# A third tile of an expert with at most 64 rows, run as 64 rows with both parts in one stationary block

## The chip, the core and the metric

The kernel runs on one core of one Trainium2 chip. The metric is the device time in microseconds (us) of one execution, as the median of several runs. The engines are called PE (TensorE: matmuls, with PEld its weight loads), ACT (ScalarE), DVE (VectorE), POOL (GpSimd) and SP (SyncE, which here issues DMAs). Each has a queue of its own and takes its instructions in order; they wait for each other through semaphores. A matmul multiplies a stationary block (up to 128 x 128) with a moving block of up to 512 columns and adds the result up in PSUM.

## What is computed

A clustered attention (8 heads, 2 batches, 768 tokens, 64 values per head: each query sees only the keys of its own cluster), and on its 1536 result rows of 512 values a mixture of 8 experts with a hidden layer of 1024. Each row goes to the expert of its largest logit; an expert takes at most 384 rows (capacity). Cut to the second half:

```python
logits = x @ w_gate                       # x: 1536 x 512, w_gate: 512 x 8
expert_idx = np.argmax(logits, axis=1)
# row i is put at the next free place of its expert's queue, if there is one
h = np.maximum(np.einsum('ecd,edf->ecf', disp, w1), 0.0)     # 512 -> 1024
y = np.einsum('ecf,efd->ecd', h, w2)                         # 1024 -> 512
out[i] = gate_w[i] * y[expert_idx[i], pos[i]]
```

How many rows an expert gets depends on the data. In the input that is timed, the eight counts are 198, 119, 169, 188, 162, 192, 206 and 302.

## The kernel before

Products are made to near float32 precision by splitting each operand into two 12-bit parts, high and low, and adding three products: high x high, high x low and low x high. So each block of an expert's product is three matmuls.

An expert's rows lie in up to three tiles of 128 rows (`ST` = 3). Two of them (`MT` = 2) are always computed, together: `gemm1` makes the hidden layer in 8 groups (one for each `f`, 12 matmuls of 256 columns each, weights stationary, lines 733 to 748), `gemm2` makes the result of one tile of 128 rows (24 matmuls of 512 columns, the hidden layer stationary, line 674). The third tile is wanted only by an expert with more than 256 rows; it stands behind a branch on the count (line 831) and is computed by `single`: 4 transposes of the rows (`turn`, line 644, with ACT at line 646 writing the high part and DVE at line 647 the low one), 24 matmuls of 512 columns for the hidden layer (line 702, with the rows as the stationary block), two turns of the hidden layer (4 transposes each), 24 matmuls for the result (line 674), and `finish`: DVE scales the rows with the gate's weight (line 667), and POOL scatters them to the output (line 527). Expert 0 is special: its first tile is closed early and computed before the routing is done, so it has a fourth tile, and two branches. In the timed input only expert 7 has a third tile, with 302 - 256 = 46 rows; all other branches are passed over.

The counts are fetched into registers of all engines by `values_load` (line 813), one load per expert and engine. The weights come in chunks of 0.5 MB by DMA and are split by ACT (line 126) and DVE (line 132); `w_next` does so between the groups of matmuls.

The order of the work in the experts' part is that of a scheduler, within the stretches between barriers. It also places the branches: that of an expert stands, in PE's queue, between the expert's `gemm1` and its `gemm2`. The seven loads of the counts of experts 1 to 7 follow behind the two branches of expert 0 and 24 more matmuls.

Of the kernel before, what the change touches and what calls it, by code (L numbers as in the profile page):

```python
# [7 lines left out]
F32 = mybir.dt.float32  # L8
R32 = mybir.dt.float32r
BF16 = mybir.dt.bfloat16  # L10
I32 = mybir.dt.int32
AF = mybir.ActivationFunctionType
ALU = mybir.AluOpType
# [3 lines left out]
P = 128  # L17
BIG = float(2 ** 60)
# [5 lines left out]
def kernel(  # L24
# [13 lines left out]
    nc = tc.nc  # L38
    B, NP, _, S = qT.shape
# [65 lines left out]

    # ---- expert weights: 0.5 MB chunks, each split into two 12-bit parts
    slots = [wra.tile([P, 2, 1024], R32, name=f"ws{c}") for c in range(NA)]
# [25 lines left out]

    # Scores are two products, K = 112 and 97: W x Y1 and Qs x Y0.
    #   main rows:  q_hi x k_hi              | q_hi x k_lo
    #   piece rows: q_lo x k_hi, d 0-31      | q_lo x k_hi, d 32-63
    #   last rows:  query x key cluster mask | -(row maximum) x 1
    # for heads of parity 0; mirrored for parity 1, whose rows 16-31 and 1-31 are zero
    MAIN = (slice(0, 64), slice(64, 128))
# [32 lines left out]

    # ---- cluster assignment of the two heads of a pair -> 0/1 rows for W, 0/-BIG rows for Y1
    cl = {}
# [15 lines left out]
    def cl_scores0(nm, t0=0, t1=NT):  # L190
        # first pair: centroids as they came, all heads' at once; each product leaves its own 32 columns
        # and the next one writes over the rest
        if t0 == 0:
            cl[0, nm] = psS.tile([P, 512], F32, tag="s", name="ctp")
        for t in range(t0, t1):
            nc.tensor.matmul(
                out=cl[0, nm][:, t * 32:(t + NP) * 32],
                lhsT=pair[0][nm][:, t * P:(t + 1) * P],
                rhs=cbr,
                start=True,  # L200
                stop=True,
            )

    def cl_assign(pi, mul=nc.gpsimd, norm=None, nm="qk"):
        # token x (tile, q/k, head) groups; pair 0: one call each for q and k
        G = NT * 2 * len(nm)
        tv = (cl.pop(pi) if norm is None else cl.pop((pi, nm)))[:, 0:G * 16]
        if norm is not None:
            sn = work.tile([P, NT * 4, 16], F32, tag="csn", name="csn", bufs=2)[:, 0:G]
            nc.vector.tensor_tensor(  # L210
                out=sn.rearrange("p (t g) c -> p t (g c)", g=2),
                in0=tv.rearrange("p (t c) -> p t c", c=32),
                in1=norm.to_broadcast([P, NT, 32]),
                op=ALU.mult,
            )
            tv = sn
        else:
            tv = tv.rearrange("p (g c) -> p g c", c=16)
        mx = work.tile([P, NT * 4, 1], F32, tag="cmx", name="cmx")[:, 0:G]
        nc.vector.tensor_reduce(out=mx, in_=tv, axis=AX.X, op=ALU.max)  # L220
        yield
        eq = work.tile([P, NT * 4, 16], BF16, tag="ceq", name="ceq", bufs=2)[:, 0:G]
        nc.vector.tensor_tensor(out=eq, in0=tv, in1=mx.to_broadcast([P, G, 16]), op=ALU.is_equal)
        c16 = c16b.rearrange("p (o c) -> p o c", o=1)
        mul.tensor_tensor(out=eq, in0=eq, in1=c16.to_broadcast([P, G, 16]), op=ALU.mult)
        yield
        m2 = work.tile([P, NT * 4, 1], BF16, tag="cm2", name="cm2")[:, 0:G]
        nc.vector.tensor_reduce(out=m2, in_=eq, axis=AX.X, op=ALU.max)
        yield
        # the groups of 16 (q even, q odd, k even, k odd head) go to columns 0, 32, 64, 96  # L230
        g0, ng = 2 * "qk".index(nm[0]), 2 * len(nm)
        ov = ohb.rearrange("p t (g c) -> p t g c", c=32)[:, :, g0:g0 + ng, 0:16]
        nc.vector.tensor_tensor(
            out=ov,
            in0=eq.rearrange("p (t g) c -> p t g c", g=ng),
            in1=m2.rearrange("p (t g) o -> p t g o", g=ng).to_broadcast([P, NT, ng, 16]),
            op=ALU.is_equal,
        )
# [28 lines left out]

    # ---- exact split of q and k into two 12-bit parts
    ql = {}
# [25 lines left out]

    # ---- row maxima of the masked scores, per query
    mxt = {}
# [24 lines left out]
    def max_part(h, j, pool=psO, tag="o"):  # L322
        # maxima of half the queries, transposed one tile at a time
        mx = work.tile([P, TH], F32, tag="mxp", name="mxp")
        ts = slice(j * TH, (j + 1) * TH)
        nc.vector.tensor_tensor(out=mx, in0=mxt[h][:, 0, ts], in1=mxt[h][:, 1, ts], op=ALU.max)
        br = MROW[h % 2]
        tp = pool.tile([P, 512], F32, tag=tag, name="mtd")
        if j == 0 and h == 0:
            keep_warm(WARM2, tp)  # L330
        for t in range(TH):
            nc.tensor.transpose(tp[0:1, t * P:(t + 1) * P], mx[:, t:t + 1], ident)
        nc.scalar.activation(
            out=pick(Qs_t, h)[br:br + 1, j * HALF:(j + 1) * HALF], in_=tp[0:1, 0:HALF], func=AF.Copy, scale=-1.0
        )
        if j == 1:
            mxt.pop(h)
# [10 lines left out]

    # ---- attention proper
    pt = {}  # L350
# [78 lines left out]

    # ---- routing: expert, gate weight, position in the expert's queue; rows go to their slots  # L430
    run = []

    def gate(b, t0=0, t1=NT):
# [18 lines left out]
        yield  # L452
        # positions in the queues, and positions + first rows of the experts' slots
        ps = psT.tile([P, 512], F32, tag="t", name="gps")
# [4 lines left out]

        # earlier rows of the same tile, earlier tiles, earlier calls  # L460
        o2 = oh.rearrange("p (o t) e -> p o (t e)", o=1).to_broadcast([P, 2, n * E])
# [6 lines left out]
        nc.tensor.matmul(out=pv, lhsT=oneb, rhs=spread(run[-1], n), start=False, stop=True)  # L468
        # gate weight of the largest logit: 1 / (sum exp(l - max) + 1e-9)
        ex = tl("gex")  # L470
        nc.vector.tensor_tensor(out=ex, in0=lg, in1=mx.to_broadcast(sh), op=ALU.subtract)
        nc.scalar.activation(out=ex, in_=ex, func=AF.Exp)
        # slot out of range when the expert is full
        v, w = tl("gv"), tl("gw")
# [11 lines left out]
        for t in range(n):  # L486
            scatter("xd", xd, si[:, t], xt[b][:, t0 + t, :], (E * ST + 1) * P - 1)
        # tokens of each expert so far, per row
        cnew = tl("gcu", E, F32, 1)[:, 0]
# [8 lines left out]
    def first_rows():  # L498
        # expert 0's first tile takes no rows after this: later ones start at its second
        ebr, dlr = (const.tile([P, E], BF16, name=n) for n in ("ebr", "dlr"))  # L500
        nc.vector.memset(ebr, 0.0)
        nc.vector.memset(dlr, 0.0)
        nc.vector.tensor_copy(ebr[0:1], cs[0:1, C_EB:C_EB + E])
        first.append(ebr)
        run0 = const.tile([P, E], BF16, name="run0")
        nc.vector.memset(run0, 0.0)
        run.append(run0)
        first.append(dlr)
# [16 lines left out]
    def scatter(key, dst, idx, src, bound):  # L525
        # rows of one call never meet those of another: no order among the calls
        i = nc.gpsimd.indirect_dma_start(  # L527
# [26 lines left out]
    def hooks(i, g):  # L554
# [13 lines left out]
        if i == 0:  # L568
# [4 lines left out]
            if g in (2, 3, 4, 5):  # L573
                split(2, g - 2)
        # work for other heads between the groups of head i
        n = i + 1
# [39 lines left out]

    # ---- experts
    def moe(tail):
# [20 lines left out]
        def turn(src, hi, lo, pool, tag):  # L639
            # [rows, n * 128] -> n blocks of [128, rows], in two 12-bit parts  # L640
            tp = pool.tile([P, 512], F32, tag=tag, name="rtp")
# [39 lines left out]

        # one tile of 128 rows: both products with the rows stationary, the hidden layer turned between them
        def single(e, t, sfx, pools):
# [28 lines left out]
            for f in range(KF):  # L712
# [4 lines left out]
                gemm2_step(ps, e, f, h[0], h[1], slice(0, P))  # L717
            finish(e, t, ps, sfx)

        hf0 = []  # L720
# [50 lines left out]
        for e in range(E):  # L771
# [58 lines left out]
            for t in range(2 if e == 0 else MT, T0 if e == 0 else ST):  # L830
                with tc.If(n_e[e] > t * P):  # L831
                    for _ in single(e, t, "c", one):
                        pass

    def keep_warm(n, d):
        # the tensor engine's clock rises only while it is busy; nothing reads these products
        for _ in range(n):
            nc.tensor.matmul(out=d[:, 0:P], lhsT=onef, rhs=onef, start=True, stop=True)

    def centroid_scale():  # L840
        # 1 / (|c| + 1e-6) on every partition; the root is refined by one Newton step
        nc_ = NP * 32
# [144 lines left out]
def _prepare(inputs):  # L987
# [12 lines left out]
    t["v1"] = vv  # L1000
    # centroids, block-diagonal for the two heads of a pair
    cp = c.reshape(H // 2, 2, 16, D)
# [46 lines left out]
```

## Time and profile before

| | us |
|---|---|
| median of 3 runs | 513.41 |
| lowest and highest run | 513.39, 515.55 |
| profiled execution: span from first to last instruction | 508.1 |
| PE busy in it | 478.8 |
| DVE busy in it | 376.2 |
| ACT busy in it | 318.2 |
| POOL busy in it | 149.5 |

The span is that of one profiled execution; the device time has 5.3 us more, which lie outside of it. The experts' part is the last 200 us or so of the span. A row of a time line gives the start and the duration of an instruction, its engine and its line; several alike in a row are one row with a count (x2), and the duration is then that of all. Matmuls overlap: one of 512 columns is shown with 0.39 us, and the next starts 0.23 us behind it. In square brackets stands the idle time of the engine ahead of it, and what ended it. `PEq` is PE's sequencer, which also does loads of registers and branches.

### The profile page before, as it was taken

The page shows a single profiled execution, that of the slowest core. Times are in us where ns is not written, and L with a number is a line of the kernel's source. Part 1 is how long each engine was busy: PE and PEld are TensorE (multiplying, and loading weights), DVE is VectorE, ACT ScalarE, POOL GpSimd, SP SyncE. Part 2 cuts the span into 40 slices and gives each one's busy share as a digit, 9 for nine tenths or more (in the row PEclk, how much of TensorE's full clock was granted, in tenths as well). Part 3 has the DMA queues.
Part 4 walks back from the last instruction along what each step waited for, and adds up shares of the span by engine and source line. Part 5 has one row for each costly group of instructions (what it writes and reads, how often), then busy time and mean ns, then how long its engine had stood idle before and what let it go on. Part 6 is the DMA issues. An engine that isn't in the chain of part 4 may idle for free. (4 is left out here: it accounts for less than half of the span.)

```text
span 508.1 us, 8328 instructions
## 1 busy us (share of the span) xinstructions
PE 478.8 (94%) x2921; PEld 413.3 (81%) x2921; DVE 376.2 (74%) x649; ACT 318.2 (63%) x642; POOL 149.5 (29%) x122
## 2 busy tenths in 40 slices
PE   7789999999999989899999999999999999999994
PEld 7657879789888778798888767889898989898873
DVE  4897997898879889999996775575756566675411
ACT  5386787786977978779788825464545546372410
POOL 7676444536532475244100040000000010101001
PEclk9799999999999999999999999999999999999998
DMA  8435749686241452332101058685858494755001
GB/s 242 130 69 144 247 126 332 212 264 204 60 128 49 126 191 58 81 90 55 51 2 42 1 181 317 210 265 189 281 182 295 139 307 165 270 178 182 0 9 41
DMA packets 31152, 77.69 MB, mean 153 GB/s; under 512 B 4710, under 2 KB 5056, under 8 KB 31106
## 3 DMA queue, kind: packets, MB, share of 16 engines
q1 hardware_dynamic: 26162, 60.94, 39.3%
q0 software_dynamic: 4944, 16.15, 8.4%
q8 instruction: 27, 0.44, 0.4%
q14 instruction: 19, 0.16, 0.1%
HBM read 50.07 MB, written 17.45 MB: 133 GB/s over the span
## 5 line engine op out<-in xcount | busy, mean ns | idle before, releaser
L370 ACT ACTIVATE pf<-s 128x384 f32<-128x384 f32 x192 | 94.6, 493 | 50.1 <-PE s L362 36.8
L313 DVE TENSOR_REDUCE mx<-m 128x1 f32<-128x384 f32 x192 | 101.8, 547 | 17.3 <-PE m L306 16.1
L376 DVE TENSOR_TENSOR pl<-pf,ph 128x768 fp32r<-128x768 f32 x88 | 101.7, 1156 | 10.1 <-ACT ph L370 8.5
L132 DVE TENSOR_TENSOR ws<-wraw,ws 128x1024 fp32r<-128x1024 f32 x64 | 78.7, 1248 | 24.7 <-ACT ws L126 24.6
L370 ACT ACTIVATE ph<-s 128x384 fp32r<-128x384 f32 x192 | 94.3, 491 | 0.0
L742 PE MATMUL g<-xh,ws 128*128 128x256 f32 x448 | 80.5, 282 | 0.0
L674 PE MATMUL g<-ws,hh 128*128 128x512 f32 x240 | 76.6, 400 | 1.6 <-PEq L831 0.8
L126 ACT ACTIVATE ws<-wraw 128x1024 fp32r<-128x1024 f32 x64 | 66.0, 1052 | 19.3 <-DMA wraw<-in_w_dram 15.4
L306 PE MATMUL m<-Y,W 112*128 112x384 f32 (+1 forms) x192 | 68.5, 362 | 5.2 <-DVE mx L313 4.7
L527 POOL DMA_INDIRECT out_dram<-y,row x17 | 16.5, 972 | 187.3 <-DVE y L667 135.8
L742 PEld LDWEIGHTS g<-xh,ws 128*128 128x128 f32 x448 | 69.6, 190 | 1.1 <-DVE hl L747 0.4
L387 PE MATMUL o<-pl,vh 128*65 128x384 f32 x192 | 65.6, 342 | 4.7 <-DVE pl L376 4.5
L361 PE MATMUL s<-W,Y 112*128 112x384 f32 (+1 forms) x192 | 68.6, 358 | 0.4 <-ACT ph L370 0.4
L362 PE MATMUL s<-Qs,Y 97*128 97x384 f32 (+1 forms) x192 | 65.0, 344 | 1.4 <-DMA Qs<-mr 1.3
L387 PE MATMUL o<-ph,vh 128*65 128x384 f32 x192 | 65.3, 340 | 0.0
L387 PE MATMUL o<-ph,vl 128*65 128x384 f32 x192 | 65.3, 340 | 0.0
L742 PE MATMUL g<-xl,ws 128*128 128x256 f32 x224 | 63.1, 282 | 0.0
L746 ACT ACTIVATE hh<-g 128x256 fp32r<-128x256 f32 x56 | 21.4, 385 | 60.7 <-PE g L742 59.0
L674 PEld LDWEIGHTS g<-ws,hh 128*128 128x128 f32 x240 | 43.5, 188 | 11.6 <-issue 1.9
L674 PE MATMUL g<-ws,hl 128*128 128x512 f32 x120 | 47.3, 394 | 0.5 <-DVE hl L647 0.5
L306 PEld LDWEIGHTS m<-Y,W 112*128 112x128 f32 (+1 forms) x192 | 37.0, 194 | 13.0 <-DVE mx L313 10.9
L284 POOL TENSOR_TENSOR ql<-qv,W 64x768 fp32r<-64x768 f32 x16 | 31.2, 1952 | 52.6 <-ACT W L282 34.3
(182 smaller groups left out, 769.6 us busy)
## 6 DMA issues: line engine op xcount, KB each, us to landing
wraw<-in_w_dram SPq DMA_DIRECT2D x64, 512.0 KB
row<-xd SPq DMA_DIRECT2D x25, 260.0 KB
xd<-z POOLq DMA_DIRECT2D x7, 780.0 KB, 5.2
v<-in_v_dram SPq DMA_DIRECT2D x8, 390.0 KB
qv<-in_qT_dram SPq DMA_DIRECT2D x8, 384.0 KB
kv<-in_kT_dram SPq DMA_DIRECT2D x8, 384.0 KB
Y<-Y SPq DMA_DIRECT2D x32, 96.0 KB
Qs<-W SPq DMA_DIRECT2D x16, 192.0 KB
```

The lines of the kernel that those rows point to most:

```text
L126: nc.scalar.activation(out=w[:, 0], in_=raw[c], func=AF.Copy)
L132: nc.vector.tensor_tensor(out=w[:, 1], in0=t, in1=w[:, 0].bitcast(F32), op=ALU.subtract)
L284: nc.gpsimd.tensor_tensor(out=ql[h][a], in0=d["q"][a], in1=W[a].bitcast(F32), op=ALU.subtract)
L306: nc.tensor.matmul(out=m[:, 0:HALF], lhsT=W[0:KA[h % 2], t * P:(t + 1) * P], rhs=Y1[0:KA[h % 2], j * HALF:(j + 1) * HALF], start=True, sto ...
L313: nc.vector.tensor_reduce(out=mxt[h][:, j, t:t + 1], in_=m[:, 0:HALF], axis=AX.X, op=ALU.max)
L361: nc.tensor.matmul(out=s[:, 0:HALF], lhsT=Y1[0:ka, ks], rhs=W[0:ka, qs], start=True, stop=False)
L362: nc.tensor.matmul(out=s[:, 0:HALF], lhsT=Y0[0:kb, ks], rhs=Qs[0:kb, qs], start=False, stop=True)
L370: nc.scalar.activation(out=o[:, g % 2], in_=s[:, 0:HALF], func=AF.Exp, scale=1.0 / float(D) ** 0.5)
L376: eng.tensor_tensor(out=pl, in0=pf, in1=ph.bitcast(F32), op=ALU.subtract)
L387: nc.tensor.matmul(out=ot[h, j][0:VW, 0:HALF], lhsT=lhs, rhs=r, start=(kt == 0 and n == 0), stop=(kt == NT - 1 and n == 2))
L674: nc.tensor.matmul(out=ps[:, 0:DM], lhsT=h[:, f, ts], rhs=w[:, a, fs], start=(f == 0 and n == 0), stop=(f == KF - 1 and n == 2),)
L742: nc.tensor.matmul(out=ps[:, 0:w_], lhsT=w[:, a, fs], rhs=x[e][:, k, :], start=(n == 0), stop=(n == 3 * KD - 1))
```

## The change

The branch for a third tile gets a second one inside it. With more than 64 rows in the tile, `single` runs as before. With 64 or fewer, a new function `halved` runs. It transposes 64 rows, and writes high and low part of each block side by side, 64 columns each, so that one stationary block of 128 columns holds both. A block of the product is then two matmuls: `wide` (128 stationary columns with the weights' high part) and `low` (the 64 columns of the high part with the weights' low part). The upper 64 rows of the result in PSUM hold the products of the low part; `folded` copies them down with ACT and adds them to the others with DVE, once for each half of the hidden layer and once for the result. The rectification of the hidden layer moves into the turn (`turn_hidden`). The result is scaled by DVE and scattered by POOL. Comments fall away.

```diff
+        def halved(e, t, pool, tag):
+            HP = P // 2
+            (x, _), (h, _), hf = alloc("c")
+            x, h = (v.rearrange("p k (a n) -> p k a n", a=2) for v in (x, h))
+            hf = hf[0:HP]
+            UW = min(FF, 512)
+
+            def turn_half(src, dst, relu):
+                tp = pool.tile([P, 512], F32, tag=tag, name="rtp")
+                n = src.shape[1] // P
+                for k in range(n):
+                    nc.tensor.transpose(tp[:, k * HP:(k + 1) * HP], src[:, k * P:(k + 1) * P], ident[0:HP, 0:HP])
+                tv = tp[:, 0:n * HP].rearrange("p (k n) -> p k n", k=n)
+                hi, lo = dst[:, :, 0, :], dst[:, :, 1, :]
+                nc.scalar.activation(out=hi, in_=tv, func=AF.Relu if relu else AF.Copy)
+                if relu:
+                    nc.vector.scalar_tensor_tensor(
+                        out=lo, in0=tv, scalar=0.0, in1=hi.bitcast(F32), op0=ALU.max, op1=ALU.subtract
+                    )
+                else:
+                    nc.vector.tensor_tensor(out=lo, in0=tv, in1=hi.bitcast(F32), op=ALU.subtract)
+
+            def turn_hidden(u):
+                fs = slice(u * UW // P, (u + 1) * UW // P)
+                turn_half(hf[:, u * UW:(u + 1) * UW], h[:, fs], True)
+
+            def step(ps, v, w, i, last, width):
+
+                def wide():
+                    lhs = v.rearrange("p a n -> p (a n)")
+                    nc.tensor.matmul(out=ps[:, 0:width], lhsT=lhs, rhs=w[0], start=(i == 0), stop=(i == last))
+
+                def low():
+                    nc.tensor.matmul(out=ps[0:HP, 0:width], lhsT=v[:, 0], rhs=w[1], start=False, stop=False)
+
+                for go in (wide, low) if i < last else (low, wide):
+                    go()
+
+            def folded(ps, dst, width):
+                s0 = pools[-1].tile([P, DM], F32, tag="y", name="y", bufs=3)[0:HP, 0:width]
+                nc.scalar.activation(out=s0, in_=ps[HP:P, 0:width], func=AF.Copy)
+                nc.vector.tensor_tensor(out=dst, in0=ps[0:HP, 0:width], in1=s0, op=ALU.add)
+
+            r = rows.pop((e, t))
+            turn_half(r[0:HP, 0:DM], x, False)
+            for u in range(FF // UW):
+                us = slice(u * UW, (u + 1) * UW)
+                ps = pool.tile([P, 512], F32, tag=tag, name="g1")
+                for k in range(KD):
+                    if u > 0 and k == KD // 2:
+                        turn_hidden(u - 1)
+                    w = wsl[8 * e + k]
+                    step(ps, x[:, k], (w[:, 0, us], w[:, 1, us]), k, KD - 1, UW)
+                folded(ps, hf[:, us], UW)
+            ps = pool.tile([P, 512], F32, tag=tag, name="g2")
+            for f in range(KF):
+                if f == (2 if FF > UW else 0):
+                    turn_hidden(FF // UW - 1)
+                w = wsl[8 * e + 4 + f // 2]
+                fs = slice((f % 2) * DM, (f % 2 + 1) * DM)
+                step(ps, h[:, f], (w[:, 0, fs], w[:, 1, fs]), f, KF - 1, DM)
+            y, z = (pools[-1].tile([P, DM], F32, tag="y", name="y", bufs=3)[0:HP] for _ in range(2))
+            folded(ps, y, DM)
+            nc.vector.tensor_scalar(out=z, in0=y, scalar1=r[0:HP, DM:DM + 1], scalar2=None, op0=ALU.mult)
+            scatter("out", out, r[0:HP, DM + 1:DM + 2].bitcast(I32), z, NTOK - 1)
...
                 with tc.If(n_e[e] > t * P):
-                    for _ in single(e, t, "c", one):
-                        pass
+                    kept = rows[e, t]
+                    with tc.If(n_e[e] > t * P + P // 2) as more:
+                        for _ in single(e, t, "c", one):
+                            pass
+                    rows[e, t] = kept
+                    with more.Else():
+                        halved(e, t, *one[0])
```

The scheduler places the longer branches elsewhere. PE at the two branches of expert 0, before (`g_4068` is the result of expert 0's second tile, `g_4407` and `g_4427` are the first two groups of expert 1's `gemm1`; `ci` holds the counts):

```order
L831 UNCONDITIONAL_BRANCH x2
L674 MATMUL g_4068<-ws_3923,hh 128x512 x2
L674 MATMUL g_4068<-ws_3923,hl 128x512
...
L742 MATMUL g_4407<-xh,ws_4008 128x256 x2
L742 MATMUL g_4407<-xl,ws_4008 128x256
L813 TENSOR_LOAD ci x7
L742 MATMUL g_4427<-xh,ws_4005 128x256 x2
```

And with the change, where line 880 is the loads, 898 and 900 are the outer and the inner branch, `g_4561` and `g_4581` are expert 1's first two groups:

```order
L674 MATMUL g_4068<-ws_3924,hl 128x512
L809 MATMUL g_4561<-xh,ws_4005 128x256 x2
...
L809 MATMUL g_4561<-xl,ws_4008 128x256
L880 TENSOR_LOAD ci
L898 COMPARE_AND_BRANCH
L900 COMPARE_AND_BRANCH
...
L900 UNCONDITIONAL_BRANCH
L898 UNCONDITIONAL_BRANCH
L880 TENSOR_LOAD ci x7
L809 MATMUL g_4581<-xh,ws_4005 128x256 x2
```

What stood between the branches and the seven loads, the end of `g_4068` and expert 1's first group, now stands ahead of the branches; the loads follow directly behind the second branch. The other branches move in the same way: that of expert e, which stood ahead of its `gemm2`, now stands behind it and behind the first group of expert e + 1.

PE at expert 7, before (`g_6497` is its last group of `gemm1`, `g_6513` and `g_6543` its two `gemm2`, between them and it the third tile):

```order
L742 MATMUL g_6497<-xl,ws_4008 128x256
L831 COMPARE_AND_BRANCH
L644 MATMUL rtp<-cs,row 128x128 x4
L702 MATMUL g_6586<-ws_4005,xhc 128x512 x2
...
L674 MATMUL g_6621<-ws_113,hlc 128x512
L831 UNCONDITIONAL_BRANCH x2
L674 MATMUL g_6513<-ws_110,hh 128x512 x2
...
L674 MATMUL g_6543<-ws_113,hl 128x512
L1045 UNCONDITIONAL_BRANCH
```

And with the change (`g_7159` is the second `gemm2`, `g_7238` belongs to `single`, `g_7287` and `g_7318` to `halved`):

```order
L674 MATMUL g_7159<-ws_113,hl 128x512
L898 COMPARE_AND_BRANCH
L900 COMPARE_AND_BRANCH
...
L674 MATMUL g_7238<-ws_113,hlc 128x512
L900 UNCONDITIONAL_BRANCH
L732 MATMUL rtp<-cs,row 128x64 x4
L751 MATMUL g_7287<-ws_4005,xhc 128x512
L754 MATMUL g_7287<-ws_4005,xhc 64x512
...
L754 MATMUL g_7318<-ws_113,hhc 64x512 x2
L751 MATMUL g_7318<-ws_113,hhc 128x512
L900 UNCONDITIONAL_BRANCH
L898 UNCONDITIONAL_BRANCH
```

The third tile, which stood ahead of both `gemm2` of expert 7, now stands behind them, at the end of PE's work; its matmuls alternate between 128 and 64 stationary columns.

## Rows read from the trace of the kernel before

**Rows 1.** The page, part 1: busy us, share of the span, instructions.

```profile
PE 478.8 (94%) x2921; PEld 413.3 (81%) x2921; DVE 376.2 (74%) x649; ACT 318.2 (63%) x642; POOL 149.5 (29%) x122
```

**Rows 2.** By stretch: us; busy PE, PEld, DVE, ACT, POOL; clock, DMA, GB/s.

```profile
310.00:330.00 20.00, 18.72 (x116) 15.90 (x115) 12.69 (x16) 11.26 (x18) 0.97 (x1) 1.00 0.72 237
330.00:476.00 146.00, 145.11 (x944) 131.06 (x944) 94.48 (x125) 73.60 (x111) 11.66 (x12) 1.00 0.64 214
```

**Rows 3.** PE at expert 0's branches, time line: start us, us, engine, line, op.

```profile
317.35 0.60 PE L644 MATMUL rtp<-cs,row 128*128 128x128 f32 x4
318.70 0.71 PE L674 MATMUL g<-ws,hh 128*128 128x512 f32 x2 [0.75 <-PEq L831]
```

**Rows 4.** Time line of PE around the branch of expert 1.

```profile
333.53 0.28 PE L742 MATMUL g<-xl,ws 128*128 128x256 f32 x1
333.96 0.70 PE L674 MATMUL g<-ws,hh 128*128 128x512 f32 x2
```

**Rows 5.** Instructions of line 813: count, ns min/median/max, first and last start.

```profile
L813 PEldq TENSOR_LOAD <-ci x7: 300/306/313, 320.2 to 322.6; - x7
```

**Rows 6.** Time line of PE at the end of those loads.

```profile
322.85 0.28 PE L742 MATMUL g<-xl,ws 128*128 128x256 f32 x1
323.00 0.47 PE L742 MATMUL g<-xh,ws 128*128 128x256 f32 x2
```

**Rows 7.** Busy time by stretch, columns as in rows 2, early stretches.

```profile
15.30:22.10 6.80, 5.95 (x30) 5.56 (x30) 5.78 (x14) 3.06 (x4) 5.90 (x7) 0.50 0.63 170
...
35.80:39.20 3.40, 3.40 (x12) 2.94 (x12) 2.52 (x4) 2.51 (x7) 0.78 (x1) 0.50 0.52 111
```

**Rows 8.** Time line of PE: the matmuls behind two of its pauses.

```profile
16.15 0.63 PE L243 MATMUL ctq<-idb,ohb 128*64 128x128 bf16 x4 [3.08 <-DVE ohb L233]
...
35.05 0.39 PE L387 MATMUL o<-pl,vh 128*65 128x384 f32 x1 [1.13 <-DVE pl L376]
```

**Rows 9.** Time line of all engines: the third tile's entry and end.

```profile
476.07 0.60 PE L644 MATMUL rtp<-cs,row 128*128 128x128 f32 x4
...
476.76 0.60 ACT L646 ACTIVATE xhc<-rtp 128x512 fp32r<-128x512 f32 x1
477.39 0.69 DVE L647 TENSOR_TENSOR xlc<-rtp,xhc 128x512 fp32r<-128x512 f32 x1 [0.28 <-ACT xhc L646]
...
477.41 0.73 PE L702 MATMUL g<-ws,xhc 128*128 128x512 f32 x2 [0.73 <-ACT xhc L646]
...
489.42 0.63 PE L674 MATMUL g<-ws,hhc 128*128 128x512 f32 x2
...
490.12 0.63 PE L674 MATMUL g<-ws,hh 128*128 128x512 f32 x2
```

**Rows 10.** Groups of one shape from 440 us: busy us, mean ns.

```profile
L747 DVE SCALAR_TENSOR_TENSOR hl<-g,hh 128x256 fp32r<-128x256 f32 x16 | 6.8, 422 | 6.3 <-ACT hh L746 6.0 <-ACTq L831 0.3
...
L746 ACT ACTIVATE hh<-g 128x256 fp32r<-128x256 f32 x16 | 6.2, 385 | 17.5 <-PE g L742 16.9
```

**Rows 11.** Time line of all engines at the kernel's end.

```profile
501.09 0.39 PE L674 MATMUL g<-ws,hl 128*128 128x512 f32 x1
501.52 0.75 DVE L667 TENSOR_SCALAR y<-g,row 128x512 f32<-128x512 f32 x1 [4.85 <-PE g L674]
502.54 0.97 POOL L527 DMA_INDIRECT out_dram<-y,row  x1 [4.62 <-DVE y L667]
```

**Rows 12.** Time line of PE: a matmul with 6 stationary columns.

```profile
59.02 0.34 PE L306 MATMUL m<-Y,W 128*128 128x384 f32 x1
59.19 0.34 PE L387 MATMUL o<-ph,vh 128*65 128x384 f32 x1
59.37 0.27 PE L344 MATMUL mtp<-cs,mxx 128*6 128x128 f32 x1
59.39 0.42 PE L387 MATMUL o<-ph,vl 128*65 128x384 f32 x1
59.65 0.34 PE L387 MATMUL o<-pl,vh 128*65 128x384 f32 x1
```

## Prediction

> **What bounds the kernel now.** I began with the page's busy times: TensorE (PE) is busy for 478.8 of 508.1 us, no other engine comes near [rows 1]. Such a share is a mean over stages, so the second view is busy time by stretch. From 330 to 476 us, where the experts run, PE works 145.11 of 146.00 us at a granted clock of 1.00 [rows 2]. There a matmul taken away shortens the kernel by its pitch, and a stop of PE that nothing covers lengthens it by as much. The last 30 us are different: what counts is when the last product leaves GpSimd (POOL). The third view, the time line of PE, gives the places that the change touches: the two branches of expert 0 (PE idle 0.75 us [rows 3]), a branch of a later expert that isn't taken (0.15 us: a matmul that ends at 333.81, the next at 333.96 [rows 4]), and the one third tile that runs. In this input only expert 7 has more than 256 rows (302, so 46 in the third tile); the trace shows only one such pass, at 476.07 to 490.12 [rows 9].
>
> **Part 1: the halved tile.** 48 matmuls of 512 columns become 32. Three of them take 0.70 us (489.42 to 490.12 [rows 9]), so the pitch is 0.233 and PE is relieved of 16 x 0.233 = 3.73 us. What eats into this is that the tile has moved: the order now has it behind both second products of expert 7, as the kernel's last work, where nothing covers its folds. I go through it from 476.07.
> - The two second products come first: 48 x 0.233 = 11.20, to 487.27.
> - Entry. Four transposes at a pitch of 0.11 (0.60 for four, of which the last is 0.27), then ScalarE (ACT) writes the high part and VectorE (DVE) the low one, with the shapes of 128x256: 0.385 and 0.422 [rows 10]. A stationary block now holds both parts, so the first matmul waits for both: 0.33 + 0.27 + 0.09 + 0.385 + 0.03 + 0.42 + 0.03 = 1.55 us (the 0.09 and 0.03 are the steps between engines at 476.67 and 477.36 [rows 9]). Before, the first matmul came 1.34 us after the transposes' start. First matmul at 488.82.
> - 32 matmuls, 7.47 us; two turns of the hidden layer, 4 x 0.11 = 0.44 each.
> - Two waits for those turns. From a last transpose's start to the first product that uses it the steps above are 1.22 us. Behind the first turn stands one matmul (0.11 + 0.233 = 0.34 of cover, 0.88 of wait); behind the second stand four (1.04 of cover, 0.18 of wait).
> - So PE issues until 488.82 + 7.47 + 0.88 + 1.06 = 498.23; its last matmul starts at 498.00 and ends at 498.39. Before it was 501.09 and 501.48 [rows 11]: 3.1 us sooner.
> - The tail. Before: DVE scales 0.04 us after the matmul, POOL starts the scatter at 502.54, 1.06 us behind PE [rows 11]. After: ACT copies the low half (0.60, as its 128x512 form takes at 476.76 [rows 9]; an estimate for 64 partitions), DVE adds (0.69, as at 477.39), DVE scales, POOL. With steps of 0.09, 0.03, 0.06 and 0.27 that is 0.09 + 0.60 + 0.03 + 0.69 + 0.06 + z + 0.27 = 1.74 + z. z reads SBUF where its old form reads PSUM (0.75); no row shows it, so 0.40 to 0.75: 2.1 to 2.5 us, POOL at 500.5 to 500.9. **Gain 1.6 to 2.0 us; I take 1.8.**
>
> **Part 2: the register loads.** The count of each expert is fetched into registers by one load per engine. On PE seven of them stand in a row, each 306 ns, from 320.2 to the last one's start at 322.6 [rows 5]: about 2.74 us. Now they cost nothing, because 24 matmuls were handed to PE ahead of them: the last of them starts at 322.85 and the first one behind the loads at 323.00 [rows 6]. The cover is only just enough. In the new order the same 24 matmuls stand ahead of expert 0's branches, and the loads right behind them. A branch that isn't taken waits until PE has finished its own work: that is the 0.75 us of idle PE [rows 3]. So behind it PE holds nothing, and the seven loads pass with PE still: 7 x 0.306 plus the steps between them, 2.74, and up to 0.6 to fill the queue again as after a branch. **Loss 2.75 to 3.4 us; I take 2.8.** No work can be pulled up from behind, since an engine's queue keeps its order. Nor is it given back: PE has 0.9 us of idle time left in the 146 us that follow [rows 2]. ACT, DVE and SP have their loads there too; they wait for PE's next group anyway.
>
> **Part 3: the clock.** PE will now be still for 0.75 + 2.8 = 3.5 us in one piece, in the middle of dense work. Two rows show what such a pause does. After one of 3.08 us (to 16.15 [rows 8]) the granted clock was 0.50, the 1.2 GHz level, from 15.30 to 22.10, with 5.95 us of busy PE in it [rows 7]: half of that, 3.0 us, was lost. After one of 1.13 us (to 35.05 [rows 8]) it was 0.50 from 35.80 to 39.20, PE busy all along: 1.7 us lost. The pause of 0.75 us left no mark: the stretch around it has a clock of 1.00 [rows 2]. 3.5 us is longer than both that did. PE is dense before and after, as in the second case, so nearer to 1.7. **Loss 1.7 to 3.0; I take 2.0.** If the level stayed, 0.
>
> **Part 4: what costs nothing or little.** The other branches are only passed over: 0.15 us each as before [rows 4]. They jump over more code now; at worst each costs what the first two did, 0.375, which is 8 x 0.22 = 1.8 us more. I take 0 and keep this for the upper end. Expert 1's first group now comes ahead of the branch instead of behind it: same matmuls. Rows of later experts are loaded by SP behind its branches, one product later than before; they are wanted a whole expert (some 20 us) later.
>
> **Sum.** On the profiled execution's 508.1 us: -1.8 + 2.8 + 2.0 = +3.0, 511.1. The median is 5.3 us above the span, which lies outside of it and stays: 513.4 + 3.0 = **516.4 us**.
>
> **The rivals.**
> 1. The clock holds. Everything else as forecast: 513.4 - 1.8 + 2.8 = 514.4. For it: the pause of 0.75 us did nothing. Against: 1.13 us already did. Chance 0.17; it decides between "same" and "slower".
> 2. Each change between a stationary block of 128 columns and one of 64 stops PE. The low products have 64, and they alternate with the wide ones, so there are up to 32 changes. The price if a matmul must run out first: its 0.39 less the pitch of 0.233, 0.16 x 32 = 5.1 us, so 516.4 + 5.1 = 521.5. Against it stands a matmul with 6 stationary columns between ones of 65 and 128 [rows 12]: from 59.19 to 59.65 PE issues it and two matmuls of 384 moving columns, whose pitch is 0.17 (59.02 to 59.19). That leaves 0.46 - 0.34 = 0.12 for it, where a transpose of its 128 moving columns has 0.11. No stop is to be seen. Chance 0.08. The Trainium skill, TensorEngine Tiling (Array Packing), section Key Properties, says: "Changing tiling mode (not just tile) drains the TensorE". If the widths of 64 and 128 are two such modes, the time is this rival's; the 6 columns of rows 12 show no drain.
> 3. Faster: the loads stay hidden, as they are now [rows 6], since the branch lets PE keep a queue. Then neither part 2 nor part 3 happens: 513.4 - 1.8 = 511.6, or 511.4 at best; that is on the better side, still within 0.5%. To pass 0.5% the tail would have to cost no more than before too (513.4 - 3.1 = 510.3). Against: the 0.75 us at the branches is PE standing empty [rows 3]. Chance 0.07, of which 0.02 below 510.84.
> 4. The change doesn't do what it says: the third tile has over 64 rows and runs as before, moved to the end. Its 48 matmuls and its end are those of today, so nothing is won: 513.4 + 2.8 + 2.0 = 518.2. The 46 rows come from the counts; chance 0.02.
>
> **How the numbers follow.** Forecast 516.4, chance 0.66: its terms give -2.0 + 2.75 + 1.7 = +2.45 at the low end and -1.6 + 3.4 + 3.0 = +4.8 at the high end, 515.9 to 518.2. A measurement of this kernel can tell some 0.5% (2.57 us) from no change; so "slower" begins at 515.98, and the forecast sits just above it. The range must take in rival 1 (-2.0 + 2.75 at its lower end, 514.2) and a part of the jumps of part 4: 513.9 to 518.6. Left out are rivals 2 and 3, 0.15, and little else. Faster by over 0.5%: 0.02. Within 0.5%: rival 1, the rest of rival 3 and what of the forecast ends below 515.98 (0.14): 0.36. Slower: the rest of the forecast, rivals 2 and 4: 0.62.
>
> **What will show it.** In the trace of the changed kernel: a still PE of 3 to 3.6 us around 322 to 326 with seven loads in it (part 2; under 1 us and rival 3 holds). A granted clock of 0.50 for 3.4 to 7 us right behind it (part 3; 1.00 throughout and rival 1 holds). The third tile from its transposes to its last matmul in some 11.1 us (12 or less is right; 16 means rival 2), waits of 0.9 and 0.2 us in it, and POOL's last scatter 2.1 to 2.5 us behind the last matmul. What would make the prediction wrong: a pause elsewhere that the order doesn't show, above all at the jumps over the longer branches.

## The result and the profile after

The changed kernel takes 517.75 us in the median of 20 runs (514.49 to 522.09), the kernel before 513.81 us in 20 runs of its own (510.73 to 518.95). The ratio is 1.0076, with a 95% interval of 1.0058 to 1.0093: 3.9 us slower, 3.0 to 4.8.

The profiled execution of the changed kernel has a span of 519.2 us, against 508.1. That difference of 11.1 us isn't all the change's: each run of the list is 1.8 us longer than its own span (521.02 and 519.2 here), so that the one profile is of an execution 3.3 us above its median, and the other of one some 3.9 us below its own. 6.4 us of the 11.1 lie ahead of the place that the change touches, in code that both share (expert 1's first matmul starts at 327.22, before at 321.53, of which 0.75 were the branches'); a part of it is one wait of 2.20 us for a row's load and a clock of 0.51 behind it. So I compare stages, not spans.

The first row is from the time line of PE (start us, us, engine, line), the second from the table of busy time by stretch (us; busy PE, PEld, DVE, ACT, POOL; granted clock):

```profile
312.57 0.67 PE L644 MATMUL rtp<-cs,row 128*128 128x128 f32 x2 [2.20 <-DMA row<-xd]
...
312.60:316.10 3.50, 3.50 (x11) 2.93 (x12) 0.21 (x1) 1.30 (x2) 0.00 (x0) 0.51 1.01 363
```

The place of the loss is expert 0's branches. The time line of PE there, which answers to [rows 3, 6]:

```profile
327.22 0.40 PE L809 MATMUL g<-xh,ws 128*128 128x256 f32 x2
...
328.54 0.28 PE L809 MATMUL g<-xl,ws 128*128 128x256 f32 x1
333.80 0.77 PE L809 MATMUL g<-xh,ws 128*128 128x256 f32 x2 [4.98 <-issue]
```

PE is still for 4.98 us. What its sequencer did in that time is in the instructions of lines 880 (the loads, [rows 5]) and 898 (the outer branch): count, ns min/median/max, first and last start. The row of the loads is of the stretch from 328 to 336 us, that of the branches of the whole span.

```profile
L880 PEldq TENSOR_LOAD <-ci x7: 304/306/532, 330.7 to 333.4; - x7
...
L898 PEldq COMPARE_BRANCH  x9: 70/318/1481, 326.9 to 496.1; - x9
```

The seven loads run from 330.70 to 333.74, all of it inside the pause. Ahead of them lies something else: one of the branches took 1.48 us, from 329.01 to 330.49, where no branch of the kernel before takes over 0.34. Then the clock, by stretch:

```profile
329.00:333.10 4.10, 0.00 (x0) 0.00 (x0) 1.65 (x2) 1.29 (x2) 0.42 (x1) 1.00 0.69 236
333.10:339.90 6.80, 6.11 (x28) 6.14 (x29) 1.84 (x3) 1.71 (x3) 0.00 (x0) 0.50 0.51 153
339.90:356.00 16.10, 16.10 (x102) 14.37 (x102) 10.51 (x14) 8.68 (x13) 0.97 (x1) 1.00 0.67 217
```

Behind the pause PE is granted 0.50, the 1.2 GHz level, for 6.8 us, 6.11 of them busy: half of that, 3.1 us, is lost. The stage from the first matmul of expert 1's `gemm1` (327.22) to the last of expert 7's (488.97) takes 161.75 us where it took 154.41. The pause and the clock would make it 8.0 longer; 0.7 is given back in it. Its two ends before, and its last row with the change:

```profile
321.53 0.40 PE L742 MATMUL g<-xh,ws 128*128 128x256 f32 x2
...
475.95 0.29 PE L742 MATMUL g<-xl,ws 128*128 128x256 f32 x1
```

```profile
488.97 0.28 PE L809 MATMUL g<-xl,ws 128*128 128x256 f32 x1
```

The third tile stands at the end, as the order said, and it runs halved (lines 751 and 754 are `wide` and `low`). Its entry, with the first alternating matmuls, and its end, which answer to [rows 9, 11]:

```profile
500.38 0.46 PE L732 MATMUL rtp<-cs,row 64*128 64x64 f32 x4
...
501.82 0.50 PE L751 MATMUL g<-ws,xhc 128*128 128x512 f32 x1 [0.98 <-DVE xhc L741]
...
502.16 0.39 PE L754 MATMUL g<-ws,xhc 128*64 128x512 f32 x1
...
502.39 0.40 PE L751 MATMUL g<-ws,xhc 128*128 128x512 f32 x1
...
502.62 0.39 PE L754 MATMUL g<-ws,xhc 128*64 128x512 f32 x1
```

```profile
511.17 0.40 PE L751 MATMUL g<-ws,hhc 128*128 128x512 f32 x1
511.60 0.59 ACT L761 ACTIVATE y<-g 64x512 f32<-64x512 f32 x1 [2.67 <-PE g L751]
512.23 0.68 DVE L762 TENSOR_TENSOR y<-g,y 64x512 f32<-64x512 f32 x1 [2.84 <-ACT y L761]
512.95 0.48 DVE L784 TENSOR_SCALAR y<-y,row 64x512 f32<-64x512 f32 x1
513.70 0.92 POOL L527 DMA_INDIRECT out_dram<-y,row  x1 [11.22 <-DVE y L784]
```

From the start of expert 7's last `gemm1` matmul (488.97) to POOL's last scatter (513.70) are 24.74 us; before they were 26.59 (475.95 to 502.54). The halving gains 1.85 us, even with its folds exposed. From the transposes to the last matmul the tile takes 10.8 us, where 11.1 was forecast.

### The profile page after: what moved, and what is told of

Its sections match the earlier page's. It is cut to its first block, busy times and chain, and to the rows that moved or that the text cites. A ratio compares the mean times of both kernels' runs of the same rounds, so it can differ in the third digit from the quotient of the medians.

```text
span 519.2 us, 8323 instructions
## 1 busy us (share of the span) xinstructions
PE 482.2 (93%) x2905; PEld 416.1 (80%) x2905; DVE 378.5 (73%) x652; ACT 317.9 (61%) x643; POOL 149.6 (29%) x122
## 4 chain that ended last, share of the span: by engine, by line
issue 43%; PE 26%; DVE 12%; DMA 9%; ACT 5%; POOL 2%; POOLq 1%; another core or an unknown queue 1%; SPq 0%; ACTq 0%; DVEq 0%
PE o L387 9%; DMA xd<-x,gsi 7%; DVE pl L376 6%; PE m L306 4%; PE s L361 3%; DVE mx L313 3%; PE s L362 3%; PE otp L408 3%; PE ctp L182 2%; POOL out_dram L527 2%; ACT ph L370 2%; ACT pf L370 1%; ACT W L282 1%; DMA cs<-in_cst_dram 1%
## 5 line engine op out<-in xcount | busy, mean ns | idle before, releaser
L809 PE MATMUL g<-xh,ws 128*128 128x256 f32 x448 | 83.6, 289 | 5.9 <-issue 5.0
L809 PEld LDWEIGHTS g<-xh,ws 128*128 128x128 f32 x448 | 71.8, 196 | 7.7 <-issue 7.1
L809 PE MATMUL g<-xl,ws 128*128 128x256 f32 x224 | 64.3, 287 | 0.0
L306 PEld LDWEIGHTS m<-Y,W 112*128 112x128 f32 (+1 forms) x192 | 37.1, 194 | 13.0 <-DVE mx L313 11.1
```

Source lines behind the costliest of these rows:

```text
L306: nc.tensor.matmul(out=m[:, 0:HALF], lhsT=W[0:KA[h % 2], t * P:(t + 1) * P], rhs=Y1[0:KA[h % 2], j * HALF:(j + 1) * HALF], start=True, sto ...
L809: nc.tensor.matmul(out=ps[:, 0:w_], lhsT=w[:, a, fs], rhs=x[e][:, k, :], start=(n == 0), stop=(n == 3 * KD - 1))
```

## The experiments

My theory: the halving gains nearly what it should; the change loses because its branches, with the loads behind them, were moved to where PE has nothing queued, and because the clock falls behind the pause. The rivals: that the loss lies in the tile's new place at the end, or in the longer branches as such. All ratios are to the kernel before, in runs on the same chip as the experiment. Pauses and clocks are those of one profiled execution each.

| kernel | ratio (95%) | PE's pause at expert 0's branches and loads | clock behind it |
|---|---|---|---|
| the change | 1.0076 (1.0058 to 1.0093) | 4.98 us | 0.50 for 6.8 us |
| own_buffers | 0.9949 (0.9919 to 0.9980) | 1.80 | 1.00 |
| loads_apart | 1.0002 (0.9973 to 1.0030) | 2.97 | 1.00 |
| before_loads_behind | 1.0070 (1.0040 to 1.0100) | 3.80 | 0.50 for 3.4 us |
| nested_only | 1.0005 (0.9973 to 1.0037) | 2.12 | 1.00 |
| halved_only | 0.9957 (0.9924 to 0.9991) | 0.70 | 1.00 |
| branches_apart | 0.9946 (0.9917 to 0.9976) | 0.15, 0.15, 0.49 | 1.00 |
| clock_fill | 1.0250 (1.0189 to 1.0312) | 1.39, 0.69 | 1.00 |

**Why the branches moved: own_buffers.** In the halved tile the temporaries have the tag `y`, whose three buffers the second products use too. My explanation is that a scheduler that sees the branch wait for buffers that `gemm2` releases puts it behind `gemm2`. So I gave them other memory: the buffer that the full tile's result has, and the hidden layer's tile, which has been read by then.

```diff
-                s0 = pools[-1].tile([P, DM], F32, tag="y", name="y", bufs=3)[0:HP, 0:width]
+                s0 = pools[-1].tile([P, DM], F32, tag="yc", name="y", bufs=1)[0:HP, 0:width]
...
-            y, z = (pools[-1].tile([P, DM], F32, tag="y", name="y", bufs=3)[0:HP] for _ in range(2))
+            y, z = hf[:, 0:DM], hf[:, DM:2 * DM]
```

> The change, but the three temporaries of the halved tile no longer come from the y buffers that the second products use. In the order the branches and the seven loads then stand where they stood before the change, and the third tile ahead of the second products. Theory (the loss of the change is the exposed loads, the stop at the branches and the clock behind it; the halving itself gains): PE sheds 16 x 0.233 = 3.7 us less the longer waits at the turns, about 1.2, and the folds are covered: 2.5 us faster than before, 511.2, no pause over 1 us near 318 to 334 us, clock 1.00 there. Rival (the longer branches themselves cost, by their jumps): the pause at the branches of expert 0 is 1.9 us as in the changed kernel and the time is 513 to 515.

The ratio is 0.9949, about 2.6 us faster than before (1.0 to 4.2), as the theory had it (2.5). The branches stand again where they stood before the change, though they are as long as the change's: the buffers moved them, not their length. The loads are again behind 24 matmuls, and the clock is 1.00 through the stretch. The end of the kernel, from expert 7's last `gemm1` matmul to POOL's last scatter, takes 23.73 us, 2.86 less than before and 1.0 less than in the change, so the place at the end costs the tile 1.0 us. The rival's pause is there, though. The time line at the branches and at the end, and the busy time of the stretch around the branches (columns as above):

```profile
321.34 0.60 PE L644 MATMUL rtp<-cs,row 128*128 128x128 f32 x4
323.74 0.47 PE L674 MATMUL g<-ws,hh 128*128 128x512 f32 x1 [1.80 <-PEq L898]
...
481.04 0.28 PE L809 MATMUL g<-xl,ws 128*128 128x256 f32 x1
...
504.77 0.97 POOL L527 DMA_INDIRECT out_dram<-y,row  x1 [4.60 <-DVE y L667]
```

```profile
316.00:339.00 23.00, 20.82 (x140) 18.44 (x138) 14.07 (x19) 11.21 (x19) 0.97 (x1) 1.00 0.66 209
```

So both hold: the order decides the sign, and with the longer branches the pause is 1.05 us more than the 0.75 of [rows 3].

**The loads: loads_apart.** Each count is loaded in its own expert's first products; the branches stay where the change has them.

```diff
-                for k in range(E):
-                    n_e[k] = nc.values_load(cnt[0][0:1, k:k + 1], engines=engs, min_val=0, max_val=NTOK + P)
+                n_e[0] = nc.values_load(cnt[0][0:1, 0:1], engines=engs, min_val=0, max_val=NTOK + P)
...
                     gemm1(e, f)
+                    if f == 1:
+                        n_e[e] = nc.values_load(cnt[0][0:1, e:e + 1], engines=engs, min_val=0, max_val=NTOK + P)
```

> The change with its late branches, but each of the seven counts is loaded in the first products of its own expert, behind two groups of matmuls. Theory: 2.7 us of loads go, the pause is what the two branches take, 0.75 to 2 us, and the clock falls for 3.4 us at most: 517.8 - 2.7 - (1.4 to 3.0) = 512.1 to 513.7. Rival (the loss is the new place of the third tile, with its folds at the kernel's end): 517 to 518.

```profile
325.65 0.47 PE L809 MATMUL g<-xh,ws 128*128 128x256 f32 x2 [2.97 <-PEq L899]
...
325.50:335.50 10.00, 9.85 (x82) 9.88 (x83) 6.54 (x9) 6.31 (x10) 0.00 (x0) 1.00 0.67 212
```

```profile
478.12 0.28 PE L809 MATMUL g<-xl,ws 128*128 128x256 f32 x1
...
502.87 0.92 POOL L527 DMA_INDIRECT out_dram<-y,row  x1 [11.22 <-DVE y L784]
```

The ratio is 1.0002, some 3.8 us better than the change's on the common scale; that is 513.9 there, just above the 512.1 to 513.7 that were expected, and clear of the rival's 517. The tile stands at the end here too, with the same 24.74 us behind the last `gemm1`; so its place there isn't what makes the change lose. What is left of the pause is for the most part one branch: it took 2.54 us here. After 2.97 us of rest the clock stayed at 1.00.

**The loads and the clock without any halving: before_loads_behind.**

```diff
-                for k in range(E):
-                    n_e[k] = nc.values_load(cnt[0][0:1, k:k + 1], engines=engs, min_val=0, max_val=NTOK + P)
+                n_e[0] = nc.values_load(cnt[0][0:1, 0:1], engines=engs, min_val=0, max_val=NTOK + P)
                 for _ in b:
                     pass
+                tc.no_sync_barrier()
...
+            if e == 0:
+                tc.no_sync_barrier()
+                for k in range(1, E):
+                    n_e[k] = nc.values_load(cnt[0][0:1, k:k + 1], engines=engs, min_val=0, max_val=NTOK + P)
+                tc.no_sync_barrier()
```

> The kernel before, with the seven loads moved directly behind the two branches of expert 0; nothing is halved. Theory: a pause of 0.75 + 2.8 = 3.6 us, and a granted clock of 0.50 behind it for 3.4 to 7 us: 513.8 + 2.8 + (1.7 to 3.0) = 518.3 to 519.6. Rival (the loads cost nothing, the branches' length does): 513.8.

```profile
324.57 0.55 PE L742 MATMUL g<-xh,ws 128*128 128x256 f32 x1 [3.80 <-issue]
...
324.43:327.85 3.42, 3.28 (x15) 3.31 (x16) 1.22 (x1) 0.35 (x1) 0.00 (x0) 0.50 0.80 256
327.85:337.00 9.15, 9.15 (x79) 9.15 (x78) 5.54 (x9) 5.18 (x10) 0.00 (x0) 1.00 0.44 156
```

The barriers also move the two branches: the last 12 matmuls of expert 0's product now stand ahead of both, the 12 of expert 1's first group behind the loads, and nothing between branches and loads. The ratio is 1.0070: this alone makes the old kernel 3.6 us slower (2.1 to 5.1), a little less than I expected. The pause is 3.80 us, 3.05 more than [rows 3], and the clock is 0.50 for 3.4 us with 3.28 busy, so 1.6 us are lost; 0.7 of it comes back by the last `gemm1`, as in the changed kernel. The fall of the clock is that of one execution: the mean granted clock of this kernel's 12 executions is 0.983 in the median, as in the 35 of the kernel before beside them, so that the pause is the larger and the surer part of the 3.6 us.

**The clock by itself: clock_fill.** The same kernel, with matmuls of ones between the branches and the loads.

```diff
                 tc.no_sync_barrier()
+                keep_warm(40, psM.tile([P, 512], F32, tag="m", name="warm"))
+                tc.no_sync_barrier()
                 for k in range(1, E):
```

> The kernel before with the seven loads directly behind expert 0's branches, and 40 matmuls of ones (at a pitch of 0.11 us) put between the branches and the loads; their result is not used. They keep PE busy for 4.4 us, while the loads pass in part behind them, so that PE is still for 0.75 us, then busy, then still for 1 to 1.5. Theory (the clock falls because of the long pause): the granted clock stays 1.00 in the 10 us that follow, and expert 1's first products take 12.0 us at a pitch of 0.12 or so, where they took 1 us or more longer without the fill; the time itself is about that of the run without the fill, since the fill takes as long as it saves. Rival (it falls for the loads themselves or for the branches): 0.50 for 3.4 us or more behind the loads.

```profile
330.77 9.17 PE L845 MATMUL warm<-onef 128*128 128x128 f32 x80 [1.39 <-DVEq L831]
340.63 0.47 PE L742 MATMUL g<-xh,ws 128*128 128x256 f32 x2 [0.69 <-issue]
...
341.00:356.00 15.00, 14.85 (x112) 14.09 (x112) 8.79 (x13) 9.00 (x15) 0.00 (x0) 1.00 0.39 120
```

My size of the fill was wrong: 40 float32 products are 80 matmuls in the trace, 9.2 us and not 4.4, so the kernel is much slower (1.025), and the time tells nothing. The clock does: with the same branches and loads, but PE at rest for 1.39 and 0.69 us instead of 3.80, it stays 1.00. So the loads and the branches don't lower it by themselves. That the long pause does is what is left, shown by one execution of each kernel.

**Nesting alone: nested_only.** Both sides of the inner branch run the full tile.

```diff
-                        halved(e, t, *one[0])
+                        for _ in single(e, t, "c", one):
+                            pass
```

> The nested branch without the halving: both sides run the full tile. The order is that of before. Theory: no change, 513.8, and the branches that are passed over cost 0.15 us each as before. Rival (the longer jump costs): 0.2 us more at each of eight branches, or one stop of over 1 us at expert 0's, 515 to 516.

The order is that of before and the ratio 1.0005, so the time doesn't tell the two apart; but the trace does, for the rival. (This profile is of an execution of 520.74 us, 8.3 above the kernel's median; I read only the pause from it, which is of the kind that own_buffers shows.)

```profile
329.48 0.47 PE L674 MATMUL g<-ws,hh 128*128 128x512 f32 x1 [2.12 <-PEq L898]
```

Two branches in a row that jump over 240 PE instructions each (matmuls and weight loads, counted in the order) cost 2.12 us of rest, 1.37 more than the 120 of before in [rows 3].

**The length of the jump: halved_only.** As own_buffers, without the inner branch and the full tile (the path for a third tile of over 64 rows is left out; this input has none).

```diff
-                    kept = rows[e, t]
-                    with tc.If(n_e[e] > t * P + P // 2) as more:
-                        for _ in single(e, t, "c", one):
-                            pass
-                    rows[e, t] = kept
-                    with more.Else():
-                        halved(e, t, *one[0])
+                    halved(e, t, *one[0])
```

> As the run with own buffers, but the inner branch and the full tile inside it are gone: a third tile is always halved (enough for this input). A branch that is passed over then jumps over 88 PE instructions where own buffers has 208 and the kernel before 120. Theory (the 1.80 us at expert 0's branches is the longer jump: the second of two such jumps in a row waits for its target's instructions): the pause is 0.75 us or less, and the ratio to the kernel before 0.9949 - 1.05/513 = 0.993. Rival (the pause comes from the other engines, or from the number of branches): it stays at 1.8 us and 0.995.

```profile
322.43 0.47 PE L674 MATMUL g<-ws,hh 128*128 128x512 f32 x1 [0.70 <-PEq L898]
...
L898 PEldq COMPARE_BRANCH  x10: 70/228/339, 319.1 to 489.0; - x10
```

With 88 instructions to jump over, no branch takes over 0.34 us and the pause is 0.70, as the theory had it. The ratio, 0.9957, can't show a difference of 1 us to own_buffers: the intervals are three times as wide.

**Two jumps in a row: branches_apart.** As own_buffers, with the first of expert 0's two branches (now in a function `third`) one step earlier, 12 matmuls ahead of the second.

```diff
+                n_e[0] = nc.values_load(cnt[0][0:1, 0:1], engines=engs, min_val=0, max_val=NTOK + P)
+                third(0, range(2, T0 - 1))
+                tc.no_sync_barrier()
                 w_next()
                 next(b)
...
-            for t in range(2 if e == 0 else MT, T0 if e == 0 else ST):
...
+            third(e, range(T0 - 1 if e == 0 else MT, T0 if e == 0 else ST))
```

> As the run with own buffers, nested branch included, but the first of expert 0's two branches stands one step earlier, so that 12 matmuls of expert 0's result (2.8 us) lie between the two. Theory (the second jump waits because the first came just ahead of it): neither pause exceeds 0.4 us much, together 0.3 to 0.8 us instead of 1.80, ratio 0.992 to 0.993. Rival (any jump over so many instructions waits, and the later ones are hidden by luck): two pauses of 0.7 to 1.4 us each, 0.995 to 0.997.

```profile
319.08 0.40 PE L674 MATMUL g<-ws,hl 128*128 128x512 f32 x1
319.62 0.63 PE L644 MATMUL rtp<-cs,row 128*128 128x128 f32 x4
...
L839 PEldq COMPARE_BRANCH  x9: 70/318/2477, 314.3 to 475.4; - x9
```

The second branch still took 2.48 us, from 316.73 on, but PE was working off the 12 matmuls meanwhile and was still for 0.15 us. The pause is as the theory had it; the branch behaves as the rival said. For it waits without another jump just ahead of it, and so do branches that stand alone: here and in own_buffers those of experts 4 and 5 took 1.42 to 1.74 us, in nested_only that of expert 6 took 2.30. In own_buffers (branches from 400 to 440 us, and PE behind the first of them):

```profile
L898 PEldq COMPARE_BRANCH  x2: 1458/1598/1737, 407.8 to 431.6; - x2
```

```profile
409.82 0.28 PE L809 MATMUL g<-xl,ws 128*128 128x256 f32 x1
410.25 0.70 PE L674 MATMUL g<-ws,hh 128*128 128x512 f32 x2
```

PE had matmuls queued until 410.10 and was still for 0.15 us (0.20 in nested_only), as behind a short branch. So the wait is the branch's own and came only with the longer jumps; what it costs depends on what PE has queued ahead of it. Behind the first of two branches in a row PE has run dry, and so the second one's wait is time in full. The place of expert 0's first branch is worth about 1 us of pause (1.80 against 0.15, 0.15 and, at the loads, 0.49), which the ratio (0.9946) doesn't resolve from own_buffers.

## Why the prediction was right, step by step

The forecast of 516.4 and 515.9 to 518.2 as its own range held: on its base of 513.4 it was +3.0, and +3.9 (3.0 to 4.8) was measured.

- **The halving** (part 1): forecast 1.6 to 2.0 us gained, 1.85 measured at the end of the kernel. Inside it some steps were off and made up for each other, which was luck. Transposes of 64 rows come at a shorter pitch: 0.46 us for four, not 0.60 as in [rows 9]. The wait at the first turn of the hidden layer was 0.56, not 0.88, and that at the second is gone (no bracket in the rows between 508.05 and 509.48 of PE's time line). Against that stand steps of 0.30 to 0.34 us, where 0.233 was reckoned, at six places, five of them beside a turn or a wait. The steps of the tail stood at 0.59, 0.68 and 0.48 us, with POOL 2.13 us behind PE, at the lower end of 2.1 to 2.5.
- **The loads** (part 2): forecast 2.75 to 3.4; 333.74 - 330.70 = 3.04 us measured, and before_loads_behind shows their exposure without the halving.
- **The branches** (part 4) are the term that was mis-sized. I took 0 for the longer jumps and at worst 0.22 us each. The six that stand alone did cost 0.15 as in [rows 4], but the second of expert 0's two took 1.48 us, 1.14 more than the 0.34 of before, and 1.4 to 2.5 in the other runs with long jumps. I had spread over eight branches what falls on the one that finds PE dry. Over all nine traces: of 32 branches passed over with jumps of 88 or 120 instructions none took over 0.36 us, of 40 with jumps of 208 or 240 ten took 1.42 to 2.54. The Trainium skill, Runtime: NRT & Kernel Launch, section Instruction fetch mechanics, says that a taken branch whose target lies outside of what has been fetched waits for that block's DMA. The runs fit that: only long jumps wait, and each of the ten ended 1.35 to 1.58 us after a packet of the queue for instructions had landed, as no shorter one did. In the change that packet, 0.02 MB, falls into the 1.1 us ahead of the wait. That the branches waited for it is argued from this and not shown, and why the other 30 long jumps didn't wait stays open.
- **The clock** (part 3): forecast 1.7 to 3.0, taken as 2.0; 3.1 us in the profiled execution, of which 0.7 came back before the end of `gemm1`; 1.6 after the shorter pause of before_loads_behind. That it fell was less sure than the prediction made it, and in part luck. Of the two rows that it worked from, the second didn't have PE dense ahead of the rest (2.09 us of work in the 3.40 from 32.40 to 35.80), and it passed over a third pause of the same trace: at 191.12 PE had rested 2.97 us, and the clock stayed at 1.00. In the changed kernel the same matmul, after a rest of the same 2.97 us, is followed by 0.50 (rows below). So the length of a rest alone doesn't tell what the clock will do, and rival 1 (the clock holds), refuted here, may have been nearer than its chance of 0.17 says: with 2.97 us of rest in loads_apart it held. Over its 20 executions the change's mean granted clock is 0.974 in the median (0.969 to 0.982), that of 35 executions of the kernel before, on another chip, 0.983; that speaks for a fall in most executions, and isn't proof across two chips.
- **Rival 2** (a stop at each change of the stationary block's width): refuted. In the rows above, blocks of 128 and 64 columns follow each other at 502.16, 502.39 and 502.62, a pitch of 0.23 us, as among blocks of 128. **Rival 3** (the loads stay hidden) and **rival 4** (the tile runs in full) are refuted by the pause and by lines 751 and 754.
- **The sum** in the profiled execution: a pause 4.23 us longer, 3.1 of clock, less 0.7 given back and 1.85 gained make +4.7, against +3.9 in the median. The difference is within the interval; one execution's clock is not all executions'.
- One figure was misread without harm: I put 5.3 us outside of the span, as the difference of the median and a span of another execution. It is 1.8; since only differences were added to the median, nothing depended on it.

The pause of 2.97 us that the point on the clock speaks of, in the kernel before (PE's time line, then busy time by stretch) and with the change:

```profile
191.12 0.39 PE L387 MATMUL o<-pl,vh 128*65 128x384 f32 x1 [2.97 <-DVE pl L376]
...
191.00:198.00 7.00, 6.88 (x45) 6.01 (x46) 6.89 (x17) 5.48 (x15) 3.41 (x2) 1.00 0.16 52
```

```profile
191.91 0.39 PE L387 MATMUL o<-pl,vh 128*65 128x384 f32 x1 [2.97 <-DVE pl L376]
...
193.20:200.00 6.80, 6.80 (x27) 6.06 (x26) 4.19 (x13) 2.90 (x8) 2.20 (x2) 0.50 0.01 3
```

The packet that the third point speaks of, from the DMA view of the changed kernel from 327.9 to 329.0 us (queue: packets, MB, share):

```profile
q8 instruction: 1, 0.02, 5.7%
```

## What to carry to other kernels

Temporaries of a branch that share buffers with work outside of it tie the branch to that work: here one tag moved the branches of all experts, laid seven hidden register loads open and turned a gain of 2.6 us into a loss of 3.9. Before sizing such a change, look in the order for what PE's sequencer does behind each branch, since a branch that is passed over lets PE run dry and every load or second jump behind it is then time in full. And a pause costs twice where the clock falls behind it. At expert 0's branches rests of 1.80, 2.12 and 2.97 us left it at 1.00 and those of 3.80 and 4.98 did not; but elsewhere in the changed kernel rests of 2.20 and 2.97 us were followed by 0.50, so these runs give no length that is safe.

## What was not expected of the hardware

- A branch that jumps over 208 to 240 PE instructions can hold PE's sequencer for 1.42 to 2.54 us (ten of 40, in five kernels), where one over 88 or 120 takes 0.36 at most. With a queue ahead of it this is hidden (0.15 us of rest in branches_apart), without one it isn't.
- One product of float32 with 128 columns, which the fill used, is two matmuls in the trace at 0.11 us each.
- A stationary block of 64 columns between ones of 128 costs nothing that the trace shows: away from the turns and waits the pitch of the 32 matmuls is 0.23 or 0.24 us, but for one step of 0.30.
- The same rest of 2.97 us of PE, ahead of the same matmul, left the granted clock at 1.00 in one kernel's execution and was followed by 0.50 for 6.8 us in another's.
